# The second MLP product as seven quadrant products instead of eight in a fused attention and mixer kernel

## Chip, cores, metric

The kernel runs on one core of a Trainium2 chip. The metric is the device time of one execution in microseconds (us), taken as the median of several; a lower time is better. Each comparison with the kernel before is of runs on one chip. The runs came in three rounds on three chips (experiments 1 to 4, 5 to 8, 9 to 12), so a comparison across rounds is also one across chips; the kernel before took 242.58, 242.26 and 242.40 us there. A ratio is the mean time of one kernel's runs over that of the other's runs of the same rounds, so it is not quite the ratio of the medians that are quoted beside it.

Engine names: PE is TensorE, DVE is VectorE, ACT is ScalarE, POOL is GpSimd. L12 is line 12 of the kernel at hand, so the same operation has different line numbers in different kernels.

## The reference, cut to what matters

There are 4 batches with 8 heads, 768 tokens and 64 features per head, and so a model width of 512. Attention sees the first 8 tokens and a local window of 96. Its output x goes through a mixer of rank 32 over the tokens, and an MLP of inner width 2048.

```python
def _moe_ref(x, U, V, w_ch1, w_ch2):
    xt = x.transpose(0, 2, 1)
    h = xt @ U @ V                                    # upper mixer (U), lower mixer (V)
    u = x + h.transpose(0, 2, 1)
    ch = np.maximum(u @ w_ch1, 0.0) @ w_ch2           # first and second MLP product
    return (u + ch).astype(np.float32)
```

The second product is 768 x 2048 times 2048 x 512 per batch.

## The kernel before

The program is a list of tasks. A planner in Python gives each task an engine, a planned duration and a priority, and fixes every engine's order before anything runs. At run time each engine works through its own queue in that order and waits on semaphores. So one late operation holds up everything behind it in the same queue.

The second product adds 16 chunks of 128 inner features into one PSUM bank per 128 tokens. The residual u = x + h needs no copy of h: a small matmul of rank 32 opens the bank (called an opener here), and VectorE adds x while it evacuates.

```python
for jc in range(lo, hi_):                              # second product, 512 columns each
    nc.tensor.matmul(o, htr[:, jc, tt * P:(tt + 1) * P], w2[:, jc, c0:c1],
                     start=False, stop=(jc == NJC - 1))
...
r = slice(R * n, R * n + R)                            # openers: 32 rows of the array each, packed
nc.tensor.matmul(ps[:, banks[u].slot, 0:a1 - a0], vrep[r, t2 * P:(t2 + 1) * P], tb[r, a0:a1],
                 start=True, stop=False)
...
nc.vector.tensor_tensor(osb[go.slot][:, c0:c1], ps[:, g.slot, 0:c1 - c0], xb[:, tt, c0:c1], ALU.add)
```

The lower mixer is packed in the same way: two matmuls, each on 32 rows of the array. The scores of one pair of heads come in three packed groups.

The softmax here doesn't subtract the row's maximum and nothing guards it: scores larger than these inputs give would overflow.

Of the kernel before, what the change touches and what calls it, by code (L numbers as in the profile page):

```python
# [10 lines left out]
FP32 = mybir.dt.float32  # L11
FP16 = mybir.dt.float16  # L12
# [8 lines left out]
    "E00": 5596.5, "E01": 1664.8, "E02": 5202.8, "E03": 5286.9, "EQ0": 4669.9, "EX0.0": 1307.0,  # L21
    "EX0.1": -518.8, "EX12.0": 1114.3, "EX2.1": 975.9, "EX3.2": 537.6, "EX4.1": 1608.8, "EX8.2": 559.7,
    "HM12": 5755.8, "HM13": 2156.0, "HM14": 7019.9, "KO0": 4489.1, "NH3.2": 5312.7, "NM10": 2167.3,
    "NM3": 5298.4, "NM6": 8044.2, "PV12": 1399.7, "PV13": 1416.6, "PV6": 8196.4, "PV9": 9372.5,
    "RC3.2": 5644.0, "RS0.0": 8554.5, "RS0.2": 7675.8, "RS1.0": 7428.6, "RS1.2": 9683.1, "RS2.0": 8117.6,
    "RS2.2": 8159.2, "RS3.2": 3671.2, "S0.2": -1036.6, "S1.0": 2626.2, "S10.1": 1624.5, "S10.2": -878.9,
    "S11.0": 1624.0, "S12.0": 6395.1, "S12.2": 986.5, "S13.0": 1346.9, "S14.1": 6950.5, "S14.2": 6334.0,
    "S15.0": 8109.7, "S15.2": 2521.1, "S4.0": 8481.8, "S4.2": 7904.6, "S5.0": 7952.3, "S6.1": 7641.0,
    "S8.1": 6237.7, "S8.2": 2463.8, "S9.0": 6848.5, "S9.2": 7205.7, "SB2.0": 2581.7, "SB3.0": 6771.6,
    "SB3.1": 2983.2, "SB3.2": 8101.4, "TE0": 5574.6, "TE9": 7665.8, "TK5": 6592.9, "TQ5": 6636.0,  # L30
    "UP12": 6850.3, "UP14": -779.3, "UP3.0": -538.3, "UP4": 6846.4, "UP8": 5765.6, "VO0.0": 4489.6,
    "VO0.1": 8364.3, "VO0.2": 8500.4, "VO1.2": 4072.7, "XC0": 4148.4, "XC5": -4780.6, "back": 6420.0,
    "bias3": 6377.2, "bias5": 8633.8, "bias6": 6101.7, "bias7": 8015.2, "lk1": -5135.7, "lk14": 1912.0,
    "lk15": 6504.2, "lk2": -4615.4, "lk3": -4926.4, "lk4": 6509.6, "lk5": 1959.6, "lk6": 8451.1,
    "lk8": 6470.5, "lq1": -4643.8, "lq12": 1928.5, "lq2": -4926.9, "lq3": -4476.8, "lv0": -5269.1,
    "lv1": -5041.4, "lv2": -2399.5, "lv3": -4872.2, "mask2": 872.3, "mask3": 1688.8, "mask4": 898.2,
    "mask6": 976.9, "mask7": 898.2, "ones0": -5059.8, "ones1": -4571.4, "ones2": -5490.6, "ones3": -4531.0,
    "u16": 5397.7, "vrep0": 5597.0, "vrep1": 8031.1, "vrep2": 4679.0, "vrep3": 8452.7, "w1_0": 5521.6,
    "w1_1": -230.9, "w1_2": -4464.2, "w1_3": 7059.7,
}  # L40
CFG = {'petr': (4, 5), 'cast0': 'AD', 'E': 'DAD', 'VO': 'DPPSSSSSSSSSSSSS'}
# [19 lines left out]
class Planner:  # L61
# [42 lines left out]
    def run(self):  # L104
# [29 lines left out]
        while len(order) < len(self.tasks) and not (self.until and self.names[self.until].end):  # L134
            best = None
            for e in engines:
# [18 lines left out]
                if e == PE and t.mode and not mode:  # L155
                    s = max(s, clock[e] + self.switch)
# [48 lines left out]
def kernel(  # L205
# [17 lines left out]
    P = 128  # L223
# [20 lines left out]
    def sb(name, shape, dt, n=None):  # L244
# [9 lines left out]
    stg32 = sb("stg32", [P, 2, NB * D], FP32, 2)  # L254
    zero16 = sb("zero16", [P, 512], FP16)
    mask = sb("mask", [P, H, 384], FP16)
    bias = sb("bias", [P, H, 384], FP16)
    uf = sb("uf", [P, NB, R], FP32)
    u16 = sb("u16", [P, NB, RG, R], FP16)
    vf = sb("vf", [R, S], FP32)  # L260
    vrep = sb("vrep", [P, S], FP16)
# [3 lines left out]
    N_STG, N_V, N_QK, N_EP, N_X16, N_OSB = 3, 4, 3, 6, 3, 4  # L265
# [13 lines left out]
    osb = sb("osb", [P, DM], FP32, N_OSB)  # L279
# [4 lines left out]
        {"sq": N_STG, "sk": N_STG, "v": N_V, "kT": N_QK, "qT": N_QK, "ep": N_EP, "x16": N_X16, "osb": N_OSB, "ps": 8},  # L284
# [141 lines left out]
    def add_w1(i, prio):  # L426
        sl = slice(i * DFF // 4, (i + 1) * DFF // 4)
        c_w1.append(
            add(
                POOL, 0.78, prio, lambda: nc.gpsimd.dma_start(w1[:, :, sl], w1v[:, :, sl]),  # L430
                after=c_w1[-1] if c_w1 else loads[NP - 1][5], size=2.55, name=f"w1_{i}",
            )
        )
# [29 lines left out]
    def load_mixer():  # L463
# [11 lines left out]
    c_vrep = [  # L475
        add(DVE, 0.85, 11 + g, lambda g=g: nc.vector.tensor_copy(vrep[g * R:(g + 1) * R], vf), [c_mixl], name=f"vrep{g}")
        for g in range(RG)
    ]

    mm1_done, osb_done, ut_done, tmp_done = {}, {}, {}, {}  # L480
    m2_last = {}

    def attention(p):
# [85 lines left out]
        gkT.readers = gqT.readers = 3  # L569
        for s in range(3):  # L570
# [21 lines left out]
            def sc(s=s, gsc=gsc, lo=lo, biased=biased):  # L592
# [13 lines left out]

            SC = add(
                PE, 0.19 if s == 0 else 0.24, base + 5 + 3 * s, sc, [EQ, EK, KO, SB], margin=mg,
                lat=0.3, acq=[gsc, gep], rel=[gkT, gqT], mode=1, name=f"S{p}.{s}",
            )  # L610

# [34 lines left out]
        xw = [osb_done[b - 2]] if b >= 2 else []  # L646
# [104 lines left out]
        def hmix():  # L751
            for half in (1, 0):
                r = slice(R * half, R * half + R)
                nc.tensor.matmul(  # L754
                    ps[:, gx.slot + half, 0:HS], tmp[b % 2][r, hp * P:(hp + 1) * P],
                    vrep[r, half * HS:(half + 1) * HS], start=False, stop=True, skip_group_check=True,
                )

        HM = add(PE, 0.17, base + 26, hmix, [TE] + c_vrep, margin=mg, lat=0.3, mode=1, name=f"HM{p}")
# [21 lines left out]
    def mlp(b):  # L781
# [3 lines left out]
        relus = []  # L785
        war = [m2_last[b - 1]] if b else []
        for jt in range(NJC):
# [13 lines left out]
            def dd(hps):  # L801
# [3 lines left out]
                PE, 0.98, base + 3 * jt, mm(range(NDC - 1)), dd(range(NDC - 1)) + [c_w1[jt // 4]],  # L805
                lat=0.3, acq=[g], name=f"M1a{b}.{jt}",
            )
            Bt = add(PE, 0.33, base + 3 * jt - 1, mm([NDC - 1]), dd([NDC - 1]) + [A], lat=0.3, name=f"M1b{b}.{jt}")
# [6 lines left out]
            relus.append(add(ACT, 0.81, -10, relu, [Bt] + war, rel=[g], name=f"RL{b}.{jt}"))  # L815
        mm1_done[b] = Bt
        hN = NJC // 2
        units = [(tt, 0, DM) for tt in range(NB)]
        if b == B - 1:
            units[-1:] = [(NB - 1, 0, 3 * DM // 4), (NB - 1, 3 * DM // 4, DM)]  # L820
        firsts = [0, 2, 4] if len(units) == NB else [0, 2, 4, 5]
        banks = [Group("ps", among=MLP1) for _ in units]
        for ui, (tt, c0, c1) in enumerate(units):
                g = banks[ui]
                go = Group("osb")
                ci = 1 if c0 else 0
                nm = f"{b}.{tt}" + (f".{ci}" if ci else "")
                ahead = [u for u in range(ui, firsts[firsts.index(ui) + 1] if firsts[-1] != ui else len(units))] if ui in firsts else []

                def mm2(lo, hi_, g=g, tt=tt, c0=c0, c1=c1):  # L830
                    def go():
                        o = ps[:, g.slot, 0:c1 - c0]
                        for jc in range(lo, hi_):
                            nc.tensor.matmul(  # L834
                                o, htr[:, jc, tt * P:(tt + 1) * P], w2[:, jc, c0:c1],
                                start=False, stop=(jc == NJC - 1),
                            )
                    return go

                f = (c1 - c0) / DM  # L840
                M2 = None
                if ahead:
                    def rest(ahead=tuple(ahead)):
                        for n, u in enumerate(ahead):
                            t2, a0, a1 = units[u]
                            r = slice(R * n, R * n + R)
                            nc.tensor.matmul(  # L847
                                ps[:, banks[u].slot, 0:a1 - a0], vrep[r, t2 * P:(t2 + 1) * P], tb[r, a0:a1],
                                start=True, stop=False,
                            )  # L850

                    last_r = add(
                        PE, 0.22, base + 60 + 4 * tt + ci - 1, rest, [tmp_done[b * NP + hp] for hp in range(NP)] + [mm1_done[b]],
                        lat=0.3, acq=[banks[u] for u in ahead], mode=1, name=f"RS{nm}",
                    )
                for ch in range(4):
                    lo, hi_ = ch * NJC // 4, (ch + 1) * NJC // 4
                    dep = relus[lo:hi_] + [c_w2[ch]] + ([M2] if M2 else [last_r])
                    M2 = add(
                        PE, 0.864 * f, base + 60 + 4 * tt + ci - ch, mm2(lo, hi_), dep,  # L860
                        lat=0.3, name=f"M2{'abcd'[ch]}{nm}",
                    )
                Bt = M2

                def fin(g=g, tt=tt, go=go, c0=c0, c1=c1):
                    nc.vector.tensor_tensor(osb[go.slot][:, c0:c1], ps[:, g.slot, 0:c1 - c0], xb[:, tt, c0:c1], ALU.add)  # L866

                F = add(DVE, 0.15 + 0.55 * f, -10, fin, [Bt], acq=[go], rel=[g], name=f"F{nm}")

                def store(tt=tt, go=go, c0=c0, c1=c1):  # L870
                    nc.sync.dma_start(out[b, tt * P:(tt + 1) * P, c0:c1], osb[go.slot][:, c0:c1])
# [73 lines left out]
```

## Time and profile before

| | before |
|---|---|
| time | 242.19 us (241.71 to 242.63, 3 runs) |
| span of the profiled run | 240.6 us |
| first matmul of the first MLP product | 33.26 us |
| from there to the end of the last matmul ("the steady part") | 204.4 us |
| busy: PE, DVE, ACT, POOL | 97%, 40%, 45%, 38% |

The prediction shows the rows that carry this. Two more views are needed. The first is the slice row of the page: each digit is the busy share of one fortieth of the span in tenths, and 9 means 90% or more. The second is the table of waits: who waited for whom, us in total, times, longest.

```profile
PE   7889799999999999999999999999999999999995
```

```profile
PE ps L653 <- POOL x L739: 1.4, 2, 1.0
...
PE ps L499 <- DMA stgq<-in_q_dram: 1.2, 2, 0.8
```

After the first five slices (30 us) PE is never less than 90% busy until the last slice. Its only waits for another engine's work lie before 33 us. L653 is the upper mixer's first matmul, which needs a 16-bit copy of x that POOL casts (L739).

### The profile page before, as it was taken

The numbers are of one execution on the slowest core, as the hardware profiler recorded it, in microseconds if no ns is written. First come the engines' busy times: TensorE is split into PE (matmuls) and PEld (weight loads), VectorE is DVE, ScalarE is ACT, GpSimd is POOL, SyncE is SP. The second block draws the span as 40 slices with busy tenths as digits, with TensorE's granted clock in tenths as the row PEclk, the third lists the DMA queues.
The fourth block names the chain that finished last, engine by engine and source line by source line (L and its number), as shares of the span: only waits on it lengthen the run. The fifth ranks groups of instructions, "written<-read, shape, count | busy, mean of one in ns | idle before, by whom it ended". The sixth has DMA issues, their size and how long they took to land.

```text
span 240.6 us, 4943 instructions
## 1 busy us (share of the span) xinstructions
PE 232.8 (97%) x2092; PEld 129.8 (54%) x2092; DVE 96.7 (40%) x181; ACT 109.2 (45%) x141; POOL 91.3 (38%) x118
## 2 busy tenths in 40 slices
PE   7889799999999999999999999999999999999995
PEld 3546666566445655665545546655456456654443
DVE  5968852233364642330557852433336410001221
ACT  3786859875224028657243338567220026660000
POOL 8996994549961960190081910300001000000000
PEclk9999999999999999999999999999999999999999
DMA  8999899999999999895499996000021120000312
GB/s 172 161 181 210 114 142 199 210 174 129 159 181 196 185 161 181 117 96 38 109 155 123 142 156 157 3 0 3 2 85 48 44 87 3 0 0 4 122 53 87
DMA packets 89910, 26.39 MB, mean 110 GB/s; under 512 B 77760, under 2 KB 86912, under 8 KB 89888
## 3 DMA queue, kind: packets, MB, share of 16 engines
q0 software_dynamic: 65696, 13.24, 68.3%
q1 hardware_dynamic: 24192, 12.83, 26.2%
q8 instruction: 16, 0.26, 0.5%
q14 instruction: 6, 0.05, 0.1%
HBM read 27.46 MB, written 6.29 MB: 140 GB/s over the span
## 4 chain that ended last, share of the span: by engine, by line
PE 88%; DMA 5%; POOL 3%; DVE 2%; issue 0%; SPq 0%; POOLq 0%; DVEq 0%
PE ps L834 36%; PE ps L794 35%; PE ps L602 4%; DMA stgq<-in_q_dram 4%; PE ps L675 2%; PE ps L653 2%; PE ps L658 2%; PE ps L674 2%; PE ps L847 2%; DMA stg<-in_q_dram 2%; PE ps L754 2%; POOL x L739 1%; PE ps L895 1%; PE ps L499 1%; POOL vt L389 1%; DVE bias L340 1%
## 5 line engine op out<-in xcount | busy, mean ns | idle before, releaser
L834 PE MATMUL ps<-w,htr 128*128 128x512 f16 (+2 forms) x400 | 88.6, 371 | 0.0
L794 PE MATMUL ps<-uT,w 128*128 128x384 f16 x512 | 87.8, 326 | 0.0
L811 ACT ACTIVATE htr<-ps 128x768 f16<-128x768 f32 x64 | 51.9, 811 | 37.0 <-PE ps L794 37.0
L794 PEld LDWEIGHTS <-w 128*128 128x128 f16 x512 | 48.3, 98 | 32.0 <-issue 0.5
L613 ACT ACTIVATE ep<-ps 128x1024 f16<-128x1024 f32 (+1 forms) x48 | 44.4, 952 | 39.4 <-PE ps L602 38.0
L834 PEld LDWEIGHTS <-htr 128*128 128x128 f16 x400 | 36.1, 98 | 41.5 <-issue 3.8
L866 DVE TENSOR_TENSOR osb<-ps,x_sb 128x512 f32<-128x512 f32 (+2 forms) x25 | 16.7, 670 | 54.4 <-PE ps L834 54.2
L739 POOL CAST x<-x_sb 128x768 f16<-128x768 f32 x12 | 10.6, 888 | 53.2 <-DVE x_sb L713 25.4
L626 DVE TENSOR_TENSOR ep<-ep,mask 128x1024 f16<-128x1024 f16 x24 | 17.4, 725 | 30.6 <-ACT ep L613 30.6
L389 POOL DMA_DIRECT2D vt<-in_v_dram x16 | 16.5, 1033 | 23.7 <-PE ps L675 22.3
L296 POOL COPY vo<-vt 32x650 f16<-32x650 f16 x22 | 17.1, 782 | 6.6 <-DMA vt<-in_v_dram 6.0
L385 POOL DMA_DIRECT2D stgk<-in_k_dram x20 | 16.6, 838 | 4.1 <-DMA w<-in_moe_w_ch_dram 1.7
L385 POOL DMA_DIRECT2D stgq<-in_q_dram x20 | 16.5, 835 | 3.2 <-DMA w<-in_moe_w_ch_dram 1.7
L602 PEld LDWEIGHTS <-kT 64*128 64x128 f16 x352 | 9.9, 94 | 11.9 <-issue 10.4
L294 DVE CAST uT<-ps 128x768 f16<-128x768 f32 (+1 forms) x15 | 12.3, 845 | 8.6 <-PE ps L754 8.6
L602 PE MATMUL ps<-qT,kT 64*128 64x128 f16 x352 | 15.7, 218 | 0.0
L713 DVE TENSOR_TENSOR x_sb<-ps,rcp 128x768 f32<-128x768 f32 x16 | 15.3, 956 | 0.6
L292 ACT ACTIVATE uT<-ps 128x384 f16<-128x384 f32 (+1 forms) x5 | 2.8, 555 | 24.8 <-PE ps L754 24.8
L675 PEld LDWEIGHTS <-ep 128*128 128x128 f16 x192 | 12.4, 97 | 1.9
L675 PE MATMUL ps<-vt,ep 128*128 128x65 f16 x192 | 13.2, 193 | 0.0
L622 DVE TENSOR_TENSOR ep<-ep,mask 128x768 f16<-128x768 f16 x12 | 6.9, 573 | 14.9 <-ACT ep L613 14.9
L674 PE MATMUL ps<-vo,ep 128*128 128x65 f16 x160 | 11.9, 193 | 0.0
(57 smaller groups left out, 146.3 us busy)
## 6 DMA issues: line engine op xcount, KB each, us to landing
out_dram<-osb SPq DMA_DIRECT2D x23, 256.0 KB, 2.0
w<-in_moe_w_ch_dram POOLq DMA_DIRECT2D x8, 512.0 KB, 11.8
vt<-in_v_dram POOLq DMA_DIRECT2D x16, 192.0 KB, 8.1
stgk<-in_k_dram POOLq DMA_DIRECT2D x20, 96.0 KB, 8.7
stgq<-in_q_dram POOLq DMA_DIRECT2D x20, 96.0 KB, 7.1
vo<-vt SPq DMA_DIRECT2D x13, 121.9 KB, 6.8
stgk<-in_k_dram POOLq DMA_DIRECT2D x5, 192.0 KB, 5.1
stgq<-in_q_dram POOLq DMA_DIRECT2D x5, 192.0 KB, 5.9
```

The costliest lines, as they stand in the source:

```text
L296: nc.gpsimd.tensor_copy(dst, src)
L385: nc.gpsimd.dma_start(o[:, :, hi], src[b, h0 + hi].rearrange("(n p) d -> p n d", p=P))
L389: nc.gpsimd.dma_start(vt[gv.slot][:, :, :, 0:D], v[b, h0:h0 + 2].rearrange("h (n p) d -> p h n d", p=P),)
L602: nc.tensor.matmul(t[:, hi, j * P:(j + 1) * P], lhs, qt[r, i * P:(i + 1) * P], start=not biased, stop=True, skip_group_check=biased,)
L613: nc.scalar.activation(ep[gep.slot][:, :, lo:512], ps[:, gsc.slot:gsc.slot + 2, lo:512], AF.Exp, scale=qk_scale)
L626: nc.vector.tensor_tensor(ev, ev, mv, ALU.mult)
L674: nc.tensor.matmul(o, e[:, hi, j * P:(j + 1) * P], vof[:, hi, i - 1], start=True, stop=False)
L675: nc.tensor.matmul(o, e[:, hi, (j + 1) * P:(j + 2) * P], vv[:, hi, i], start=(i == 0), stop=True)
L794: nc.tensor.matmul(ps[:, g.slot + half, 0:HS], w1[:, dc, jt * P:(jt + 1) * P], ub[:, dc, half * HS:(half + 1) * HS], start=(dc == 0), stop ...
L811: nc.scalar.activation(htr[:, jt].rearrange("p (h c) -> p h c", h=2), ps[:, g.slot:g.slot + 2, 0:HS], AF.Relu)
L834: nc.tensor.matmul(o, htr[:, jc, tt * P:(tt + 1) * P], w2[:, jc, c0:c1], start=False, stop=(jc == NJC - 1),)
L866: nc.vector.tensor_tensor(osb[go.slot][:, c0:c1], ps[:, g.slot, 0:c1 - c0], xb[:, tt, c0:c1], ALU.add)
```

## The change

The intent is to take work from PE, which has no free time. The tokens, the inner features and the output columns are each cut into halves, so the second product becomes a 2 x 2 block product. That needs 8 block products as written, and 7 with the known rearrangement (Winograd's form of Strassen's method). The price is sums: four of activations per batch (cut into 16 instructions), four of weights once for all batches (8 instructions, called weight differences here), and more sums of the results. Besides that:

- the packed 32-row matmuls of the lower mixer and of the openers become plain full ones, padded with zeros;
- two of a pair's three score groups are merged (after the first batch);
- the results are added in place into x and stored from there.

```diff
+    sub = (nc.gpsimd if tw == POOL else nc.vector).tensor_tensor     # tw is POOL
+    if part == 0:                                                    # weights, 128x1024 each
+        sub(tB[:, 1, lo], b22, b12, ALU.subtract)
+        sub(b12, b12, b11, ALU.subtract)
+    else:
+        sub(tB[:, 0, lo], b22, b12, ALU.subtract)
+        sub(tB[:, 2, lo], b21, tB[:, 0, lo], ALU.subtract)
+    td_ = 2.3 if tw == POOL else 1.4                                 # planned, for two of them
 ...
+    nc.vector.tensor_tensor(s1, a21, a22, ALU.add)                   # activations, 128x768 each
+    nc.vector.tensor_tensor(s2, s1, a11, ALU.subtract)
+    nc.vector.tensor_tensor(a21, a11, a21, ALU.subtract)
+    nc.vector.tensor_tensor(s4, a12, s2, ALU.subtract)
 ...
+    P1 = prod(1, gX, 0, htr[:, 0:hj], w2[:, 0:hj, 0:hd], ...)        # 8 matmuls of 256 columns
+    P6 = prod(6, gX, 1, sA[:, 1], tB[:, 0], ...)
+    P7 = prod(7, gY, 0, htr[:, 0:hj], tB[:, 1], ..., c0=HS)
+    P5 = prod(5, gY, 1, sA[:, 0], w2[:, 0:hj, hd:DM], ...)
 ...                                        # copy and sums of these out of PSUM, on ACT and DVE
+    P2 = prod(2, gX, 0, htr[:, hj:NJC], w2[:, hj:NJC, 0:hd], ... + [D0])
+    P4 = prod(4, gY, 0, htr[:, hj:NJC], tB[:, 2], ... + [D2], c0=HS)
+    P3 = prod(3, gY, 1, sA[:, 2], w2[:, hj:NJC, hd:DM], ... + [D4])
 ...
+    se = POOL if CFG.get("SE", "P") == "P" and not (b == B - 1 and t == ht - 1) else DVE     # adds of shared sums into x
 ...
-    ps[:, gx.slot + half, 0:HS], tmp[b % 2][r, hp * P:(hp + 1) * P],
-    vrep[r, half * HS:(half + 1) * HS], start=False, stop=True, skip_group_check=True,
+    ps[:, gx.slot + half, 0:HS], tmp[b % 2][:, hp * P:(hp + 1) * P], vs[:, 2 * half],
+    start=False, stop=True, skip_group_check=True,
```

The second set of products, P2, P4 and P3, accumulates on top of the first in the same half bank. Each must therefore wait until the first result there has been read (D0, D2, D4). The priorities were tuned anew, so the order of the tasks differs everywhere.

## The prediction

> **What bounds the kernel now.** I read the page first (engine shares, slices), then the table of stretches, the chain that ended last in order of time, the groups by form, and the timelines of POOL and of the end. The page and the stretch from the first MLP matmul to the last matmul:
>
> ```profile
> span 240.6 us, 4943 instructions
> PE 232.8 (97%) x2092; PEld 129.8 (54%) x2092; DVE 96.7 (40%) x181; ACT 109.2 (45%) x141; POOL 91.3 (38%) x118
> PEclk9999999999999999999999999999999999999999
> ...
> 33.26:237.63 204.37, 204.35 (x1657) 111.93 (x1657) 71.31 (x124) 87.59 (x109) 62.05 (x75) 1.00 0.89 101
> ```
>
> The last line gives the length of the stretch, then PE busy: 204.35 of 204.37 us. From 33.26 us on TensorE never waits, at full clock, and every other engine has more than half of that stretch free. So after 33 us the time is the sum of what TensorE is given. As busy TensorE time is not its peak rate, I take the cost of one matmul from the chain:
>
> ```profile
> 194.41 20.80 PE ps L794 x128
> 215.21 0.32 PE ps L847 x2
> 215.53 1.83 PE ps L834 x8
> ...
> 217.68 12.19 PE ps L834 x56
> ...
> 84.62 0.27 PE ps L754 x2
> ...
> 75.90 0.33 PE ps L602 x8
> ...
> 73.57 0.50 PE ps L602 x14
> ```
>
> Columns: start, length, line, count. 128 matmuls of 384 columns take 20.80 us, so 162.5 ns each; 56 of 512 columns take 12.19, so 216 ns each once an entry of 0.1 us is taken off. Six of 128 columns (L653, L658 in the same chain) take 0.33 to 0.34, so 56 ns. A step of 0.416 ns per column joins them, and **256 columns come to 109 ns**. These 56 ns include a fresh 128x128 weight load each, so loads do not limit 256 columns either.
>
> Score groups, the mixer products (L754) and the residual openers (L847) are packed into part of the rows. Eight score matmuls in pairs should take 4 x 56 = 0.22 and take 0.33; fourteen take 0.50 instead of 0.39; after a packed group eight full matmuls take 1.83 instead of 1.73. So **each entry into and each exit from packed use costs 0.105 us**.
>
> As a check, I summed the tasks in the order the kernel issues them after 33.26: first MLP product 83.2, second 82.9 (384 x 216 ns), P times V 7.8, upper mixer 8.0, scores 7.4, residual openers 2.8, lower mixer 1.95, transposes 0.7, and 88 changes x 0.105 = 9.2. Total 204.0; the profile has 204.37. The method holds to 0.2%.
>
> Before 33 us the bounds are the loads and POOL's queue of loads and copies. The weights then arrive one chunk after another:
>
> ```profile
> 33.69 2.23 POOL L439 DMA_DIRECT2D w<-in_moe_w_ch_dram  x3
> ...
> 50.16 0.82 POOL L385 DMA_DIRECT2D stgk<-in_k_dram  x1 [1.74 <-DMA w<-in_moe_w_ch_dram]
> 52.69 1.64 POOL L385 DMA_DIRECT2D stgq<-in_q_dram  x2 [1.70 <-DMA w<-in_moe_w_ch_dram]
> ```
>
> The brackets are waits for landings: the last two chunks of the second weights land near 50.1 and 52.7, 2.5 us apart. Nothing waits for them now, because the second product starts at 59.
>
> **What the Trainium skill says.**
> - "TensorE: Matmul & The Clock Gate", Back-to-back issue gap: N/2.4 + 2.5 ns warm, 109 ns for N = 256. The trace agrees (216, 162.5, 56).
> - "TensorEngine Tiling (Array Packing)", Key Properties: "Mode switching requires drain". The trace agrees, with 0.105 us each way.
> - "GPSIMD Engine Reference", section 3.1: a two-input add of 2048 fp32 took 4497 ns against 2293 on VectorE, from one read port shared by two inputs. The trace before has no two-input POOL operation, only one-input ones (128x768 cast, 888 ns).
> - "SBUF — State Buffer": GpSimd and VectorE share a port pair as an exclusive lock, also for a VectorE operation with two SBUF inputs against a GpSimd one that reads SBUF. The trace hints at it: POOL's first x cast takes 1.13 us beside VectorE's vrep casts, and others 0.82.
>
> **The change part by part**, on TensorE after the first MLP matmul, from the changed program's order:
> - Second product: 4 batches x 3 token pairs x 7 products x 8 matmuls of 256 columns = 672 x 109 ns = 73.4 instead of 82.9: **-9.5**.
> - Residual openers: 12 groups of 4 plain matmuls of 256 columns = 5.2 instead of 2.8: +2.4. Lower mixer: 12 x 2 x 162.5 ns = 3.9 instead of 1.95: +1.95. Both stop changing mode.
> - Scores: work as before, 24 groups instead of 36.
> - One more load pair is transposed on TensorE: +0.7.
> - Mode changes: 56 instead of 88, -32 x 0.105 = **-3.4**.
>
> Sum 196.1 against 204.0: **-7.9 us**, if no wait comes in.
>
> VectorE gets, per batch, 16 sums of 128x768 fp16 (573 ns each, the row of the first mask product: 9.2 us) and 18 adds of 128x256 out of PSUM (about 425 ns, between 292 for 128 columns and 691 for 512: 7.7) in place of 6 x 691 = 4.1. That is +12.8 us per batch, about +51 in all: VectorE goes from 97 to near 145 us, about 60% busy. ScalarE gets 12 small copies (about 5 us). POOL gets 8 two-input operations of 128x1024 for the weight differences and 22 adds into x. None of these sums is the bound; each can make TensorE wait at one place.
>
> Start: VectorE loses four vrep casts and three vo copies (near 5 us) and gets four small builds; POOL has about 1 us less before the last x cast, but the first weights are issued late, behind copies. Adding POOL's durations in the new order I get the first MLP matmul at 32.5 instead of 33.3: -0.7, uncertain by 2. End: the last add is 256 columns wide instead of 128 and the last store twice as large, with more stores close together; one product near the end directly follows one into the same bank whose sibling must be read first. Together +0.8.
>
> **Rivals.**
> 1. *The weight differences come late.* TensorE's order in batch 0 has the upper mixer of pair 5 a few groups into the second product; it needs POOL's cast of pair 5, which stands on POOL behind six of the eight difference operations, and these need all of the second weights. The weights are issued later than now; counting 2.55 us per chunk in order of issue, and the delay that this count shows for the kernel before (4 us), the last two land near 57 and 60. TensorE gets there near 63.7. At the one-input rate of the trace (about 1.15 us for 1024) the cast ends near 66: a wait of 2 to 3 us, or none if the weights land as early as now. At the skill's two-input rate (2.3 us) it ends near 73: a wait near 10, a further 2 for the last difference, and perhaps a lower clock after a long gap. That gives 245 to 250. Against it: the schedule is fitted so closely (TensorE without a gap for 204 us) that its maker must have known such durations.
> 2. *VectorE becomes the pace.* In the middle batches it has about 36 us of work in 49 of TensorE, in fixed order, with operations that wait for POOL's adds and share its port. In a kernel of statically ordered queues one late operation delays all behind it. For: POOL's adds may take twice what VectorE's do. Against: 25% is free, and most products stand 0.9 us or more behind the read that frees their half bank. I put 1.5 us of scattered waits on it; were it worse, 4 to 5, giving 239.
> 3. *Nothing waits:* 242.2 - 7.9 - 0.7 + 0.8 = 234.4.
>
> **Range and chances.** The middle: 242.2 - 7.9 (TensorE work) - 0.7 (start) + 0.8 (end) + 1.5 (scattered waits) + 1.1 (my weight on the wait for the differences when POOL is quick) = **237.0 us**. The limit of 2% faster is 237.3, just above it. Rival 3 at its best, a little earlier start included, sets the low end, 233.0; a partly hidden slow POOL sets the high end, 246.0. I give 0.53 to faster by over 2%, 0.30 to within 2%, 0.17 to slower by over 2%, which needs most of rival 1.
>
> **What would show it.** Right: the second product near 8 x 109 ns per group; TensorE's work after the first MLP matmul near 196 us; groups of plain mixer products without 0.1 us on either side; VectorE near 145 us. If rival 1 holds, the table of waits shows TensorE's L-line of the upper mixer, or a product with the difference tile, waiting for POOL in batch 0, and POOL's two-input operations of 128x1024 at 2 us or more. If rival 2 holds, many short waits of products for VectorE and ScalarE reads of PSUM in the second to fourth batch. The prediction is wrong in its main step if TensorE waits more than 5 us in all after the first MLP matmul, or if a 256-column matmul with its own weights costs clearly more than 109 ns.

## The result and the profile after

The changed kernel takes **254.63 us** (254.12 to 254.99, 4 runs) against 242.24 (241.71 to 242.63, 4 runs): a ratio of 1.051, with a 95% interval of 1.048 to 1.054. It is correct and clearly slower, and lies outside the predicted range. The page and the table of stretches answer to the first fence of the prediction. The columns of a stretch are: from and to, length, busy time of PE, PEld (PE's weight loads), DVE, ACT, POOL, granted clock (the clock that TensorE was given, 1.00 is full; PEclk is the same by slices, in tenths), DMA share, GB/s. The second and third stretch are the first MLP product of batch 0, and the time from the second product of batch 0 to the first product of batch 1.

```profile
span 253.1 us, 5766 instructions
PE 230.1 (91%) x2422; PEld 165.1 (65%) x2422; DVE 149.8 (59%) x295; ACT 115.5 (46%) x156; POOL 131.1 (52%) x147
...
PE   7787999999429997799999999999999999999984
...
PEclk9999999999958999999999999999999999999999
```

```profile
34.84:249.82 214.98, 200.93 (x1980) 146.27 (x1976) 125.67 (x238) 93.28 (x122) 102.41 (x105) 0.98 0.83 98
34.84:62.81 27.97, 27.54 (x283) 16.78 (x280) 13.55 (x22) 20.80 (x28) 16.69 (x19) 1.00 1.44 192
62.81:100.86 38.05, 28.15 (x312) 23.32 (x310) 29.03 (x44) 8.43 (x12) 37.48 (x34) 0.91 1.25 106
```

PE's row has a hole of two slices, with its clock down in the second of them and in the slice behind it. The third stretch lasts 38.05 us with POOL busy for 37.48 of them and the clock at 0.91. PE is busy for 200.93 of the 214.98 us after 34.84, where it was busy in all of 204.37 before. It waited for 14.05 us there, where the prediction had named 5 us as the sign that its main step is wrong. A part of these 200.93 was done at the lower clock. The table of waits and the chain that ended last (start, length, line, count) show the hole:

```profile
PE ps L722 <- POOL x L808: 7.4, 2, 7.1
...
PE ps L864 <- DVE x_sb L956: 1.6, 1, 1.6
...
PE ps L655 <- DVE x_sb L782: 1.2, 1, 1.2
```

```profile
59.38 2.15 POOL tB L518
...
61.60 2.33 POOL w L519
63.93 2.40 POOL tB L518
...
66.40 2.33 POOL w L519
...
68.79 2.31 POOL tB L521
...
71.18 2.31 POOL tB L522
73.49 1.11 POOL x L808
74.64 0.82 PE ps L722 x6
```

L722 is the upper mixer, and L808 POOL's cast: the same pair as L653 and L739 before. Six of the eight weight differences stand before the cast in POOL's queue. Each takes 2.15 to 2.40 us, so the cast begins at 73.49. PE sat idle for 7.13 us until then. In the other two lines PE waits until VectorE has read a PSUM bank (L956 and L782 read the bank and write x). L782 stands behind two slowed sums in VectorE's queue, so the wait of L655 belongs to the differences as well. The chain's last line has the clock's price too: six 128-column matmuls took 0.82 us, and 0.51 behind a wait at full clock (29.65 us in the chain of the kernel before). VectorE's timeline for the same microseconds (start, length, line, operation, in brackets the idle time before it):

```profile
61.98 2.36 DVE L899 TENSOR_TENSOR sA<-sA,htr 128x768 f16<-128x768 f16 x1
...
66.66 2.47 DVE L903 TENSOR_TENSOR sA<-htr,sA 128x768 f16<-128x768 f16 x1
69.05 2.46 DVE L898 TENSOR_TENSOR sA<-htr 128x768 f16<-128x768 f16 x1
```

These sums of activations take 0.55 us where POOL is not at work on a difference (shown below). Beside the weight differences these three take 2.4.

What was counted on is there as well, in the chain of batch 2:

```profile
180.41 0.44 PE ps L931 x4
180.85 0.87 PE ps L943 x8
...
182.16 3.49 PE ps L943 x32
```

One product of eight 256-column matmuls takes 0.87 us, 32 take 3.49, and so one takes 109 ns. The four plain openers (L931) are followed by the product without 0.1 us between them.

The last surprise lies in front. The last of POOL's four memsets of the "ones" columns (the texts call it the third) waits for a load into another slot of the same tile, and the loads behind it wait with it:

```profile
11.52 0.15 POOL L372 MEMSET vt<- 128x12 f16 x1 [3.68 <-DMA vt<-in_v_dram]
```

The steady part begins at 34.84 us instead of 33.26.

### The profile page after: what moved, and what is told of

It is laid out like the page before. It is cut to its first block, busy times and chain, and to the rows that moved or that the text cites. A ratio compares the mean times of both kernels' runs of the same rounds, so it can differ in the third digit from the quotient of the medians.

```text
span 253.1 us, 5766 instructions
## 1 busy us (share of the span) xinstructions
PE 230.1 (91%) x2422; PEld 165.1 (65%) x2422; DVE 149.8 (59%) x295; ACT 115.5 (46%) x156; POOL 131.1 (52%) x147
## 4 chain that ended last, share of the span: by engine, by line
PE 29%; POOL 28%; issue 24%; DMA 14%; DVE 4%; ACT 0%; POOLq 0%; DVEq 0%
PE ps L943 15%; PE ps L864 8%; DMA w<-in_moe_w_ch_dram 7%; POOL vo L319 4%; POOL vt L412 4%; DMA stgk<-in_k_dram 3%; POOL stgk L408 3%; DMA vt<-in_v_dram 3%; POOL x_sb L979 3%; POOL stgq L408 2%; POOL x L808 2%; POOL w L519 2%; POOL tB L518 2%; POOL x_sb L956 1%; POOL stgk L404 1%
## 5 line engine op out<-in xcount | busy, mean ns | idle before, releaser
L881 ACT ACTIVATE htr<-ps 128x768 f16<-128x768 f32 x64 | 51.8, 811 | 30.8 <-PE ps L864 30.6
L682 ACT ACTIVATE ep<-ps 128x1024 f16<-128x1024 f32 (+1 forms) x48 | 44.2, 955 | 39.1 <-PE ps L655 38.8
L979 POOL TENSOR_TENSOR x_sb<-x_sb,u 128x512 f32<-128x512 f32 x11 | 14.4, 1311 | 44.6 <-issue 31.3
L943 PEld LDWEIGHTS <-sA 128*128 128x128 f16 x288 | 27.9, 99 | 5.3 <-issue 0.7
L956 DVE TENSOR_TENSOR x_sb<-ps,x_sb 128x256 f32<-128x256 f32 x48 | 19.5, 418 | 17.4 <-PE ps L943 9.1
L898 DVE TENSOR_TENSOR sA<-htr 128x768 f16<-128x768 f16 x16 | 12.2, 762 | 25.6 <-ACT htr L881 25.6
L943 PE MATMUL ps<-w,sA 128*128 128x256 f16 x192 | 25.3, 278 | 0.5 <-DVE x_sb L956 0.5
L943 PE MATMUL ps<-tB,htr 128*128 128x256 f16 x192 | 24.5, 272 | 1.1 <-DVE u L956 0.5
L943 PE MATMUL ps<-w,htr 128*128 128x256 f16 x192 | 24.9, 272 | 0.3 <-DVE u L956 0.2
L808 POOL CAST x<-x_sb 128x768 f16<-128x768 f32 x12 | 10.5, 876 | 20.1 <-DVE x_sb L782 12.8
L956 DVE TENSOR_TENSOR u<-ps,u 128x256 f32<-128x256 f32 x24 | 10.0, 421 | 12.4 <-PE ps L943 11.3
L655 PEld LDWEIGHTS <-kT 64*128 64x128 f16 x352 | 10.0, 94 | 11.0 <-issue 8.1
L655 PE MATMUL ps<-qT,kT 64*128 64x128 f16 x352 | 15.8, 218 | 1.3 <-DVE x_sb L782 1.2
L408 POOL DMA_DIRECT2D stgk<-in_k_dram x18 | 15.0, 841 | 3.3 <-DVE sA L898 2.2
L315 ACT ACTIVATE u<-ps 128x256 f32<-128x256 f32 x12 | 4.6, 384 | 25.5 <-PE ps L943 8.3
```

Source lines behind the costliest of these rows:

```text
L408: nc.gpsimd.dma_start(o[:, :, hi], src[b, h0 + hi].rearrange("(n p) d -> p n d", p=P))
L655: nc.tensor.matmul(t[:, hi, j * P:(j + 1) * P], lhs, qt[r, i * P:(i + 1) * P], start=not biased, stop=True, skip_group_check=biased,)
L682: nc.scalar.activation(ep[gep.slot][:, :, lo:512], ps[:, gsc.slot:gsc.slot + 2, lo:512], AF.Exp, scale=qk_scale)
L808: (nc.vector if xe == DVE else nc.gpsimd).tensor_copy(x16[gx16.slot], src)
L881: nc.scalar.activation(htr[:, jt].rearrange("p (h c) -> p h c", h=2), ps[:, g.slot:g.slot + 2, 0:HS], AF.Relu)
L943: nc.tensor.matmul(o, a[:, j, c0 + cols.start:c0 + cols.stop], bq[:, j], start=False, stop=(j == hj - 1), skip_group_check=True,)
```

## The experiments

Twelve kernels ran. "Start" is the first matmul of the first MLP product, and "steady" the length from there to the end of the last matmul, both from the profiled run's timeline (for the kernel before from its chain, 33.26; its timeline has 33.19).

| kernel | time us | ratio to before | start | steady |
|---|---|---|---|---|
| before | 242.2 to 242.6 | 1 | 33.3 | 204.4 |
| after | 254.63 | 1.051 | 34.8 | 215.0 |
| short differences (wrong) | 243.39 | 1.003 | 34.3 | 204.3 |
| differences on VectorE | 245.28 | 1.011 | 33.7 | 206.3 |
| differences and adds on VectorE | 244.09 | 1.006 | 34.5 | 204.7 |
| planned again with truer durations | 255.85 | 1.055 | 34.0 | 217.4 |
| memsets first | 242.53 | 1.000 | 33.2 | 204.3 |
| memsets first, short sums (wrong) | 240.00 | 0.990 | 32.3 | 202.4 |
| new order A | 240.05 | 0.990 | 35.2 | 199.2 |
| new order A, memsets first | 236.48 | 0.975 | 32.6 | 198.5 |
| new order B | **234.59** | **0.968** | 30.7 | 198.3 |
| new order B, differences on POOL | 248.85 | 1.026 | 30.9 | 212.3 |
| new order B, short sums (wrong) | 233.59 | 0.963 | 30.8 | 197.3 |
| before in a new order (result wrong) | 246.37 | 1.014 | 38.8 | 203.4 |

**Theory:** POOL's weight differences cost most of the loss, by holding up the cast and VectorE's sums; the arithmetic of PE's work was right. **Rivals:** VectorE's added load paces the kernel; or the seven products' dependences cost what the eighth product saves.

### 1. The differences cut short

```diff
-            b11, b12, b21, b22 = w2[:, lo, 0:hd], w2[:, lo, hd:DM], w2[:, hi_, 0:hd], w2[:, hi_, hd:DM]
+            b11, b12, b21, b22 = w2[:, lo, 0:2], w2[:, lo, hd:hd + 2], w2[:, hi_, 0:2], w2[:, hi_, hd:hd + 2]
+            tB = tBx          # a small tile; the products read slices of w2 instead, result wrong on purpose
```

> The changed kernel in its own order, but each of the eight weight differences on POOL is cut from 1024 to 8 elements per partition, and the products that read a difference read a block of the weights of the same size instead (wrong result on purpose; the same matmuls, the same order). Theory (the differences take 18 us on POOL, hold up the cast of pair 5 behind them and, by the shared port, slow VectorE's sums beside them): the waits of batch 0's second product (1.25 + 7.1 + 1.25 us), the slow clock after the long one (about 2) and the 1.6 us wait just after go, about 13 us in all: near 241.5 us, and VectorE's 128x768 sums fall from about 2.4 us to 0.6 in that stretch. Rival (VectorE with 60% load is the pace, or the late weights are): less than 4 us go, 250 or more.

Measured: 243.39 us (242.61 to 243.67). With the order and every semaphore as they were, 11.2 us of the 12.4 us loss are gone, and the steady part falls from 215.0 to 204.3. The wait for the cast is gone from the table of waits, whose first line is now

```profile
PE ps L866 <- DVE x_sb L958: 1.7, 1, 1.7
```

That is the cost of the duration of eight instructions. It is not the whole miss: the forecast was 237.0.

### 2. The differences on VectorE

```diff
-            sub = (nc.gpsimd if tw == POOL else nc.vector).tensor_tensor
+            sub = nc.vector.tensor_tensor
```

> The changed kernel in its own order, every instruction in the same place, but the eight weight differences are issued on VectorE instead of POOL (correct result). Theory (POOL's two-input rate and the lock are the cost, not the work as such): eight operations of about 0.7 us are 5.7 us more for VectorE, partly in the way; POOL's cast of pair 5 is in time; near 243 us, between 241 and 246. Rival (VectorE is the pace): VectorE's added 5.7 us cost as much or more than POOL's did, 254 or more.

Measured: 245.28 us (245.03 to 245.75), correct. The same work on the engine that already has most of the new load costs 1.9 us more than no work at all, against 11.2 us on POOL. So it is the engine and not the work.

### 3. The adds on VectorE too

```diff
-            sn = nc.gpsimd if se == POOL else V_
+            sn = V_
```

> As the previous one, and the adds into x that stand on POOL (11 of 128x512, 1.3 us each, and 11 of 128x256, 0.77 us each) are issued on VectorE too, in the same places. Theory (POOL's slow adds make VectorE, and through it TensorE, wait: VectorE waits 8 us in all for them now): 12 us more work on VectorE but no waits for POOL: about 1 to 2 us faster than the previous one, near 241.5. Rival (VectorE's load counts): slower than the previous one by 2 us or more.

Measured: 244.09 us (243.83 to 244.41), correct: another 1.2 us. PE's wait of 1.6 us for L956 at the start of batch 1 is gone. VectorE's timeline for the same sums as above:

```profile
61.43 0.55 DVE L898 TENSOR_TENSOR sA<-htr 128x768 f16<-128x768 f16 x1
62.02 0.56 DVE L899 TENSOR_TENSOR sA<-sA,htr 128x768 f16<-128x768 f16 x1
...
63.63 0.68 DVE L521 TENSOR_TENSOR tB<-w 128x1024 f16<-128x1024 f16 x1
```

A sum takes 0.55 us, and a weight difference 0.68 instead of 2.2. More load on VectorE made the kernel faster, so VectorE's pace is not the bound.

### 4. Planned again with truer durations

```diff
-    CFG = {..., 'TW': 'P'}
+    CFG = {..., 'TW': 'D'}
-            D3 = dv(se, 0.36, ...)
+            D3 = dv(se, 0.75 if se == POOL else 0.36, ...)
-            D5 = dv(se, 0.65, ...)
+            D5 = dv(se, 1.3 if se == POOL else 0.65, ...)
```

> The changed kernel with the schedule made anew: the differences on VectorE and POOL's adds entered with the durations that the trace shows (1.3 and 0.75 us instead of 0.65 and 0.36). Theory (what is lost is lost by wrong durations in the schedule): no wait of TensorE over 1 us after the first MLP matmul; stretch from there to the last matmul near 199 us against 215 in the changed kernel, the start unchanged at 34.8: near 238 us. Rival (VectorE is the pace whatever the order): waits of many small pieces stay, 243 or more.

Measured: 255.85 us (255.08 to 256.57), correct, 10.6 us slower than experiment 2, which has the same engine for the differences. That was a miss. The priorities had been tuned to the other durations. With the durations changed, the planner made another order, and PE now waits in another place: from the second product of batch 1 to the first product of batch 2 it took 38.6 us, with the clock down to 0.5 in two slices, against 28.4 in the changed kernel. Telling the truth about durations was worth nothing here without tuning the order again.

### 5. The memsets first

Base: experiment 3. The four memsets are issued at POOL's start.

```diff
+    early = [t for t in order if t.name in ("ones0", "ones1", "ones2", "ones3")]
+    order = [t for t in order if t not in early]
+    k = next(i for i, t in enumerate(order) if t.name == "iota") + 1
+    order[k:k] = early
```

> Base: the version with differences and adds on VectorE (244.09 us). Only change: GpSimd's four small memsets of the ones columns go out at its start, so that none has to wait for a load into the same tile. Theory (GpSimd's 3.7 us wait at the third memset delays the whole front, which is why the steady part began at 34.5 and not at 32.5 us): the first upper MLP product starts at 31.5 to 32.5 us, the time falls by 2 to 3 us, to 241 to 242. Rival (the front is set by the loads' own bandwidth and by the scores of the first four pairs, the memset only sits beside it): start stays within 0.5 us, time stays at 243.5 to 244.5.

Measured: 242.53 us (242.12 to 243.28), correct. It is 1.6 us faster, and the start moves from 34.5 to 33.2. The memset's wait (3.68 us in the changed kernel, 3.31 in experiment 3) was on the path of the front, but only 1.3 us of it reached PE. The expectation had the sign right and the size too large. In the kernel before, the four memsets waited for nothing, so this edit has nothing to gain there.

### 6. The memsets first and VectorE's sums cut short

Base: experiment 5. The differences and the sums of activations are cut to a few columns, as in experiment 1.

> Base: the version with differences and adds on VectorE and the memsets first. Wrong on purpose: VectorE's weight differences and its sums of activations are cut to a few columns each (same instructions, same order, same semaphores), and the products read tiles that are full, so the matmuls are unchanged in number and size. It measures what VectorE's added load costs the path in all. Theory 1 (the scattered 6 to 8 us of waits come from VectorE's added load: copies and adds behind the long sums): 4 to 6 us less than the version with the memsets first, 235 to 237. Theory 2 (they come from the order and the PSUM banks: openers and second products that wait for the copy or the add that reads the same bank before): less than 1.5 us less.

Measured: 240.00 us (239.84 to 241.14): 2.5 us less; between the two profiled runs, 0.9 in the start and 1.9 in the steady part. It lies between the two theories. The 0.9 us cannot come from the operations that were cut, which all lie behind the start; in experiment 5's profiled run the granted clock stood at 0.7 in one slice of the front, and here nowhere, but that this is the cause is not shown. So VectorE's added load of long sums costs about 2 us. The steady part is still 202.4 us, though PE's work was summed to 196.1. So about 6 us come from something else, and the order of the tasks was left. PE's timeline lists 3.85 us of them as nine waits, eight of which (3.5 us) are for VectorE's reads of half banks (L958). The rest is time in which PE counts as busy (198.6 us); where that comes from was not found.

### 7 and 8. Two new orders

Changes against the changed kernel: the differences on VectorE, planned durations as measured, the memsets given an early priority, slightly wider margins for PE's products and VectorE's adds, and the planner told that a task which opens or reuses a half bank waits for the bank's last reader and writer. The priorities were then searched anew with random steps, and two results were run. No run separates these changes from each other.

```diff
-    CFG = {..., 'TW': 'P'}
+    CFG = {..., 'TW': 'D', 'SE': 'P'}
-        switch=0.09,
+        switch=0.105,
-    D3 = dv(se, 0.36, ...)
+    D3 = dv(se, 0.78 if se == POOL else 0.38, ...)
-    D5 = dv(se, 0.65, ...)
+    D5 = dv(se, 1.32 if se == POOL else 0.7, ...)
+    if t.bank is not None:
+        r = max(r, t.bank.read + 0.1 if e == PE else t.bank.written + 0.25)
 ...                                                   # and another table of priorities
```

> A version meant to be good: the changed kernel with differences on VectorE, adds on GpSimd with their measured durations (1.32 and 0.78 us), memsets first, the planner told of each PSUM bank's last reader and writer, and its priorities searched anew. Its plan ends at 230.8; the plan of the kernel before ended at 235.2 and ran 240.6 in span, so an equal gap gives a span of 236.2, a time of 238 us. Theory (the change is worth having once the order fits the true durations): 236 to 240. Rival (the added dependences of the seven products cost what the eighth saves, whatever the order): 241 to 245.

> As the first new order, with another set of searched priorities (plan ends at 231.2 instead of 230.8). If the plan is a fair guide, within 1 us of the first new order, both 236 to 240; if chance of the order decides more than the plan, they differ by over 2 us.

Measured: order A 240.05 us (239.77 to 240.64), order B **234.59** us (234.13 to 235.59), both correct. Order B is 3.2% faster than before (ratio 0.968, 0.964 to 0.972). Its stretch after the start, and its page:

```profile
30.73:229.03 198.30, 196.93 (x1983) 146.10 (x1979) 126.97 (x249) 92.88 (x124) 86.58 (x98) 1.00 0.87 106
```

```profile
PE 223.0 (96%) x2380; PEld 162.5 (70%) x2380; DVE 149.7 (64%) x303; ACT 114.4 (49%) x156; POOL 114.6 (49%) x139
...
PEclk9999999999999999999999999999999999999999
```

PE is busy for 196.93 of 198.30 us at full clock, so its work is what the prediction had summed (196.1), within 1 us. (The sum has 56 changes of mode; counted in the timelines there are 88 before, 56 after and 51 in order B, worth 0.5 us.) VectorE is as busy as in the changed kernel (149.7 us), and PE's timeline lists 1.2 us of waits for it in that stretch. The seven products' dependences fit into this order, and so the second rival falls. The two orders differ by 5.5 us although their plans differ by 0.4, and the one with the longer plan is the faster. Most of that, 4.5 us, lies in the start (35.2 against 30.7).

### 9. New order A with the memsets first

The edit is that of experiment 5. In order A the search had moved two memsets late again, and they waited for 1.57 and 4.69 us.

> The first new order (240.05 us) with one change: the four small memsets of the ones columns go out at GpSimd's start. In its trace two of them waited 1.57 and 4.69 us for loads into other slots of the same tile, and its steady part began at 35.2 us, against 30.7 in the second new order. Theory (those waits delay the loads behind them in GpSimd's queue, and this is the whole difference of the two orders): start at 30.5 to 32, time 235 to 237. Rival (the front of the first order is late for its order of loads and casts): 239 to 240.5.

Measured: 236.48 us (235.97 to 237.06), correct, 3.6 us faster; the start moves from 35.2 to 32.6. So the memsets are most of the difference between the two orders, but not all: the start remains 1.9 us behind that of order B. In both profiled runs of order A the clock stood at 0.7 in one slice of the front, in order B's nowhere; the one run of this experiment without such a dip was its fastest, at 235.97 us, so the clock explains little of what is left.

### 10. New order B with the differences back on POOL

```diff
-            sub = (nc.gpsimd if tw == POOL else nc.vector).tensor_tensor
+            sub = nc.gpsimd.tensor_tensor
```

> The second new order (234.59 us) with one change: the eight weight differences go back to GpSimd, the place in the order unchanged. Theory (the engine is what costs: eight at 2.2 to 2.3 us each are 18 us in which GpSimd does no cast and VectorE's long sums slow down): 6 to 12 us slower, 241 to 247, with the wait of the matmuls for a cast or for a difference in batch 0 and a lower granted clock after it. Rival (the long wait of the changed kernel came from the differences standing before one cast in a bad order): within 2 us, 234.5 to 236.5.

Measured: 248.85 us (248.27 to 249.47), correct. One word costs 14.3 us, more than either theory had expected, and the good order loses all it had won. PE waits for 6.67 us for the cast, and 1.96 us for a difference, with the clock down to 0.6 in one slice:

```profile
65.26 0.82 PE L842 MATMUL ps<-ident,x 128*128 128x128 f16 x6 [6.67 <-POOL x L928]
```

Order B was tuned for differences of 0.75 us on VectorE. An order tuned for POOL's 2.2 us was not tried, so the run does not show that every order loses this much with them. The trace also tells apart two causes that always went together in the changed kernel. POOL's timeline, then VectorE's:

```profile
62.32 2.11 POOL L639 TENSOR_TENSOR w<-w 128x1024 f16<-128x1024 f16 x1
...
66.83 2.14 POOL L641 TENSOR_TENSOR tB<-w 128x1024 f16<-128x1024 f16 x1
69.06 2.31 POOL L642 TENSOR_TENSOR tB<-w,tB 128x1024 f16<-128x1024 f16 x1
```

```profile
57.92 2.35 DVE L1019 TENSOR_TENSOR sA<-sA,htr 128x768 f16<-128x768 f16 x1
66.76 0.29 DVE L936 CAST tmp<-ps 128x128 f16<-128x128 f32 x1 [6.49 <-PE ps L847]
66.97 2.43 DVE L1018 TENSOR_TENSOR sA<-htr 128x768 f16<-128x768 f16 x1
69.43 2.35 DVE L1019 TENSOR_TENSOR sA<-sA,htr 128x768 f16<-128x768 f16 x1
```

From 60.3 to 66.8 us VectorE did nothing, and POOL's difference at 62.32 took 2.11 us all the same. So 2.1 us is what POOL needs alone. From 66.8 us both are at work and alternate. POOL's L641 ends at 68.97, and the sum that VectorE had begun at 66.97 ends at 69.40, 0.43 us later. POOL's next difference ends at 71.37, and VectorE's next sum at 71.78, again 0.41 us later. Each sum ends 0.4 us after a difference does, so it seems to wait until the difference has ended. The changed kernel shows the same: its sums at 61.98, 66.66 and 69.05 us end 0.41 to 0.42 us after a difference. For the cast this interference is the small part: at 2.11 us each, six differences would take 12.7 us instead of the 13.8 that they took in the changed kernel (an estimate from these two runs). POOL's own pace is the large part.

### 11. New order B with VectorE's sums cut short

The edit is that of experiment 6.

> The second new order with VectorE's differences and sums of activations cut to a few columns, wrong on purpose, as was done to the old order, where it took off 2.5 us. Theory (VectorE's load costs the path only where the order puts a short evacuation behind long sums; in this order it does not): less than 1 us, 233.6 to 234.6. Rival (VectorE's pace costs 2 to 3 us in any order): 231.5 to 232.6.

Measured: 233.59 us (233.14 to 233.78): 1.0 us less, where the same cut took off 2.5 in the old order (there with the adds on VectorE). In the steady part VectorE is busy for 98.1 us instead of 127.0. So these 29 us of VectorE's work cost the path 1 us in a good order.

### 12. Control: the kernel before in a new order

> Control: the kernel before, unchanged but for its priorities, searched anew in the same way and for the same time as those of the changed kernel (its plan ends at 234.0 instead of 235.2). Theory (before has no waits in its steady part, so an order can only move its front and its end): 240 to 242.5, and the gain of the second new order over it stays at 5.5 to 8 us, so it is the change's. Rival (the gain comes from the search): 236 to 238.

Measured: 246.37 us (244.95 to 247.15), but the result is wrong (relative error 0.033), and so this control fails. Some order that the kernel before needs is not among the dependences that its planner knows; which one was not found. The run shows only two things. Its steady part is 203.4 us against 204.4, so a new order found hardly anything there (its timeline has 78 changes of mode instead of 88, worth 1.05 us at the prediction's 0.105). Its start is at 38.8 us, because one memset waited for 6.37 us on a load and PE then for 5.1 us, with the clock at 0.5 in one slice. How much of order B's 2.5 us in the start a correct reordering of the kernel before could have had stays open.

## Why the prediction was wrong

The prediction's own sum has five terms. The measured ones come from the table above, with the work taken as summed, since order B bears that sum out:

| term | predicted us | measured us |
|---|---|---|
| PE's work after the start | -7.9 | -7.9 taken; order B's busy PE 196.9 against 196.1 |
| start | -0.7 | +1.6 (34.84 for 33.26) |
| wait for the differences | +1.1 | +10.7 (215.0 for 204.3 in experiment 1) |
| scattered waits | +1.5 | +7.8 (the rest of the steady part, not all of it waits) |
| end | +0.8 | +0.3 (span less the last matmul's end: 3.3 for 3.0) |
| sum | -5.2 | +12.5 |

- **PE's work: right.** 109 ns for 256 columns is what 32 matmuls in 3.49 us give, plain openers have no edges of 0.1 us, the timelines have the 88 and 56 changes of mode that were counted, and order B with VectorE's sums cut short has a steady part of 197.3 us with 0.5 us of listed waits. What the change was for is there.
- **The failed step is the weight in rival 1, "my weight on the wait for the differences when POOL is quick".** The rival itself was told rightly: six differences before the cast of pair 5, near 2.3 us each (its estimate from the two-input figure), the end of the cast near 73 (measured 74.6), a wait near 10 (measured 7.1, since PE came there at 67.5 and not at 63.7), a lower clock after it. The further 2 us for the last difference did not come. The rate was taken from POOL's one-input operations (1.15 us for 1024) because the profile before has no two-input one, and the argument against was "its maker must have known such durations". The diff itself shows the contrary: it plans 2.3 us for two differences, which measure 4.5. Experiments 1, 2 and 10 settle it in two orders. In place of the 1.1 us there were 10.7. Rival 1's own forecast, 245 to 250 us, was also too low, because of the next step and of the start.
- **The second failed step is the size of the scattered waits.** Rival 2 had named them and put them at 4 to 5 us at worst; what is left of the steady part is 7.8. Not all of it is waiting: in experiment 1 PE idles for 5.1 us and counts as busy for 199.2 instead of the 196.5 that this table allows. POOL's slow adds and VectorE's sums together are 1.8 us of the 7.8 (204.3 in experiment 1, 202.4 in experiment 6). About 6 us remain with these away. Most of them are gone in orders A and B, whose steady parts are 199.2 and 198.3, and so they belong to the order of the tasks, with waits for the reads that free half banks as the part that is seen. Which of the changes that made the orders removed them, and which single dependence costs what, was not tested.
- **VectorE near 145 us: right (149.8), and it did not pace the kernel.** Moving more onto it made the kernel faster.
- **The start: wrong in sign.** Adding up POOL's durations missed the memset that waits for a load into the same tile. Experiments 5 and 9 show 1.3 and 2.6 us of it in the start.

As to what remains: order B at 234.59 us lies where rival 3, "nothing waits", put the kernel (234.4). It has a better start and waits a little more than that rival assumed, so the close agreement is in part chance.

## What to carry to other kernels

When PE has no gap, count a change in PE's own time, then go through every operation that it hands to another engine, and take that engine's duration for this form of operation, not for a similar one. If the profile has none, a published two-input rate is a better guess. A static order tuned to wrong durations must be tuned again after they are mended, and a tiny operation that shares a tile with a load belongs before the load.

## What the Trainium skill lacked or had wrong

- "GPSIMD Engine Reference", section 3.1 gives one two-input figure, for fp32, with GpSimd 1.96 times as slow as VectorE. For fp32 the runs agree: the add of 128x512 into x took 1311 ns on POOL in the changed kernel, and 683 on VectorE in order B (1.92 times). For fp16 there is no row, and the ratio is larger: a difference of 128x1024 took 2.11 us on POOL with VectorE idle, and 0.68 us on VectorE, 3.1 times.
- "SBUF — State Buffer", "Who interferes with whom", says that the second of the two engines to issue fully blocks until the first has finished. The timelines fit this, but the page does not tell what it costs when both have a queue of such operations: they alternate, and each sum of 0.55 us took 2.4 us beside differences of 2.1 to 2.4.
